# Running dense matmuls as four column groups beside P V, in a fused attention and gated-FFN block

## The chip, the cores and the metric

One core of one Trainium2 chip. The metric is the device time of one execution in microseconds; the times before are the median of three runs. Profiles are of one execution on the same core. TensorE is called PE, its weight loads PEld, ScalarE ACT, VectorE DVE, GpSimd POOL, and SyncE, which issues all DMAs, SP.

## What is computed

One transformer block on x of 2048 tokens and 1024 features, bf16: layernorm, multi-query attention with 32 heads of 32 features that share one key and one value head, a residual, a second layernorm, a gated FFN of width 3584, a second residual.

```python
q = (ln(x) @ wq)            # 2048 x 1024, 32 heads of 32
k = ln(x) @ wk              # 2048 x 32, shared by all heads
v = ln(x) @ wv              # 2048 x 32
p = softmax(q k^T / sqrt(32))
h = x + (p @ v) @ wo
g, u = ln(h) @ w_gate, ln(h) @ w_up       # 2048 x 3584 each
out = h + (sigmoid(g) * u) @ w_down
```

## The kernel before

**Tiles and stages.** Tokens go in 16 tiles of 128. Attention runs over "halves": `hf = 2 * c + hh` is token tile `c` with half `hh` of the heads (16 heads). A *visit* is one half with one tile `kt` of 128 keys; there are 32 x 16 = 512 visits, 32 for each token tile. A visit does:

- **S** (`emit_S`, L687): four matmuls that use 32 rows of the array each, at four row positions, so they run side by side ("row" mode). They write two pairs of banks of `S_ps`; there are three such pairs.
- **exp** (L707): two ACTIVATEs of 128x1024 from `S_ps` to a slot of `Pr`. S of the next visits needs the banks that earlier exps free.
- **acc add** (`make_add`, L680): DVE adds the slot to `acc`, the running sum of P over key tiles, for all halves but the first.

When enough key tiles of a half are there, **P V** (`mk_PV`, L773) multiplies them with `Vt`: for each key tile four matmuls of 32 stationary columns each, at four column positions ("col" mode), all accumulated in one bank of `F_ps`. Such a group is one *part* of the half; `parts_of(hf)` says where the parts are cut. DVE then takes the group out to `oun` (a copy for the first part, L803, an add for each later one, L807). **SUM** (`mk_SUM`, L737) reduces `acc` to row sums with 32 short col-mode matmuls of 64 columns; the reciprocal goes through `r_scratch` in DRAM and comes back to all partitions as `rb`. `OT` is `oun` times `rb` (L765).

The rest of PE's work is "dense" matmuls that use the whole 128x128 array and one of the two banks of `F_ps`: K, V and Q projections (`mk_KV`, `mk_Qc`, `mk_Q`), the output projection (`mk_OP`, L864), gate and up (`mk_GU`, L966: groups of 8 matmuls of 512 columns; for the first and last token tile, 32 matmuls of 128 columns with the weights stationary) and down (`mk_D`, L1044: two groups of 28). Gate ends in a tanh on ACT (L989), up in a multiply on DVE (L1010 or L996).

**Order.** Nothing is ordered by hand on PE. A planner (`Plan`, L48 on) runs when the program is built: it keeps a model of every engine's time and fills PE's list operation by operation. `pe_op` (L447) adds a price `SWITCH` when an operation's mode differs from the one before it; `t_act` (L159) prices an ACTIVATE. The main loop asks, in this order: is the next S known to be ready and ACT close to running dry (`run - t < TUNE["run"]`); if PE is in col mode and S will be ready within `swait`, wait for it; may a P V, SUM, OP or layernorm-transpose group interrupt the current long dense group (if at least `rmin` ns of that group are left); else the next matmul of the current group; else a new group by the priority list `PRIOS`. `in_row(few)` (L734) is the gate of P V and SUM: they begin only in row mode, that is, right after an S, or when few slots are free.

All PE instructions other than layernorm transposes are recorded by one helper, so they stand at L445.

**After the last exp.** With no S left, PE runs the rest alone: the last P V and row sums, the last output projection, gate/up of the last token tile, and the last down groups.

The row-mode gate that the change touches:

```python
def in_row(few):
    return v_done[0] >= NV or pl.pe_mode == "row" or len(free_slots) <= few or TUNE["col_ok"] and pl.pe_mode == "col"
```

Of the kernel before, what the change touches and what calls it, by code (L numbers as in the profile page):

```python
# [17 lines left out]

TUNE = dict(early=240, look=500, ln_v=1, warm=70, late=300, ws0=1, ws1=1, parts0=3, parts1=4, lord=2, h_ord=2,
            ho=3, ho2=0, pvl1=0, pvl2=0, col_ok=0, pace0=310, swait=400, parts=2, raw=1, rl=0, nd=2, pc=16,  # L20
            rate=315, pace=265, xd=4, qf=1, dall=1, wo_late=1, nkn=3, few=0, rmin=900, hmin=1, h0=100, h1=250,
            hf=1.35, run=700, sum_few=0, pv_few=4, d_off=0, d_a=-1, d_b=1, eb=450, eq=1500)


# [134 lines left out]
def t_act(n):  # L159
    return dict(occ=n / 1.2 + 58.0, lat=n / 1.2 + 186.0 + SEM)  # L160

# [4 lines left out]

SWITCH = 108.0


def bass_sequential_preLN__grouped_kv_mqa__glu_gated_glu__prompt_kernel(  # L170
# [31 lines left out]
    with ExitStack() as es:  # L202
# [238 lines left out]
        head = [["xT", "KV", "Q0"], ["KV", "Q0", "xT"], ["Q0", "KV", "xT"], ["KV", "xT", "Q0"]][TUNE["h_ord"]] + ["PV", "SUM", "OP", "hT"]  # L441
        PRIOS = [head + ["GU", "D", "Q1", "Q"], head + ["Q1", "Q", "GU", "D"], head + ["Q1", "GU", "Q", "D"]]

        def mm(o, l, r, start, stop, **kw):
            return lambda: PE.matmul(o, lhsT=l, rhs=r, start=start, stop=stop, **kw)  # L445

        def pe_op(fn, n, mode, deps, last_of_round=True):  # L447
            if mode != pl.pe_mode:
                pl.free["pe"] += SWITCH
                pl.pe_mode = mode  # L450
            if mode == "dense":
                occ = max(25.0, n / 2.4 + 2.4)
            else:
                occ = max(25.0, n / 2.4 + 2.4) - 10.5 if last_of_round else 3.5
            return pl.op("pe", fn, deps, occ=occ, lat=max(25.0, n / 2.4 + 2.0) + 170.0 + SEM)
# [51 lines left out]
        def mk_KV(t0, k):  # L507
            n = k * P
            blk, o = t0 // 4, (t0 % 4) * P

            def atoms(b):
                r = []
                for dt in range(DT):
                    r.append((mm(F_ps[:, b, 0:n], wk4[:, dt, :], xnT[:, blk, dt, o:o + n], dt == 0, dt == DT - 1),
                              n, "dense", rep_ops if dt == 0 else []))
                for x in range(k):
                    for dt in range(DT):
                        r.append((mm(F_ps[:, b, 256 + x * DH:256 + (x + 1) * DH],
                                     xnT[:, blk, dt, o + x * P:o + (x + 1) * P], wv_sb[:, dt, :],
                                     dt == 0, dt == DT - 1), DH, "dense", [wv_ld] if dt == 0 else []))  # L520
                return r

            def after(b, last):
                blk_done(blk, last)
                fa, fd = both(kT4[:, t0 * P:t0 * P + n], F_ps[:, b, 0:n])
                ke = evac(fa, fd, n, [last], 1, bias=TUNE["eb"])
                fa, fd = both(Vt[:, t0:t0 + k, :], F_ps[:, b, 256:256 + k * DH].rearrange("p (a b) -> p a b", a=k))
                ve = evac(fa, fd, k * DH, [last, ke], 2, bias=TUNE["eb"])
                for t in range(t0, t0 + k):
                    k_ev[t], v_ev[t] = ke, ve  # L530
                return [ke, ve]
            return Group("KV", atoms, lambda: [xT_ev.get(t0), xT_ev.get(t0 + k - 1), rep_ops[-1], wv_ld], after)
# [27 lines left out]
        def mk_Qc(c, qd):  # L560
            def atoms(b):
                return [(mm(F_ps[:, b, k * P:(k + 1) * P], wq_sb[:, qd, dt, k * P:(k + 1) * P],
                            xnT[:, 0, dt, c * P:(c + 1) * P], dt == 0, dt == DT - 1), P, "dense", [])
                        for k in range(2) for dt in range(DT)]
# [11 lines left out]
        def mk_Q(g, tok, n):  # L576
            def atoms(b):
                return [(mm(F_ps[:, b, 0:n], wq_sb[:, g // 2, dt, (g % 2) * P:(g % 2 + 1) * P],
                            xnT[:, tok // 512, dt, tok % 512:tok % 512 + n],
                            dt == 0, dt == DT - 1), n, "dense", []) for dt in range(DT)]  # L580
# [75 lines left out]
        def s_known(v, t):  # L656

            sd = s_ready(v)
            return sd is not None and known(sd, t) and (v < 1 or known([exps[2 * v - 2]], t + TUNE["early"]))

# [61 lines left out]

        PARTS = [(), (), (0, 8, 16), (0, 5, 10, 16), (0, 6, 11, 16), (0, 4, 8, 12, 16), (0, 7, 16), (0, 6, 16), (0, 4, 10, 16), (0, 4, 8, 16)]

        def parts_of(hf):
            return PARTS[TUNE["parts" if hf > 1 else "parts0" if hf == 0 else "parts1"]]

# [6 lines left out]
        def in_row(few):  # L734
            return v_done[0] >= NV or pl.pe_mode == "row" or len(free_slots) <= few or TUNE["col_ok"] and pl.pe_mode == "col"

        def mk_SUM(hf):  # L737
            a = acc[:, hf % 2, :]

            def atoms(b):  # L740
                return [(mm(F_ps[DH * j:DH * (j + 1), b, 0:64], sel[:, bb, :], a[:, j * 512 + bb * 64:j * 512 + (bb + 1) * 64],
                            bb == 0, bb == 7, tile_position=(0, DH * j)), 64, "col" if j == 3 else "col-", [])
                        for bb in range(8) for j in range(4)]

            def after(b, last):
# [9 lines left out]
                return [rc]  # L755
            return Group("SUM", atoms, lambda: [add_op.get((hf, NT - 1)), c_sel], after, lambda: in_row(TUNE["sum_few"]))

# [15 lines left out]
        def mk_PV(hf, part, sums=False):  # L773
# [38 lines left out]

            lag = TUNE["pvl2"] if final else TUNE["pvl1"]

            def first():
                return [exp_of[(hf, kt, i)] for kt in kts[:len(kts) - lag] for i in range(2)] + [c_one if sums else v_ev.get(kt) for kt in kts]

            def gate():
                if part == 0 and hf >= 2 and not (hf - 2 in ot_ev and known([ot_ev[hf - 2]], pl.free["pe"])):
                    return False  # L820
                if sums and part == 0 and hf >= 2 and hf - 1 not in ot_ev:
                    return False
                return (hf in RAW or all((hf, max(kt, 1)) in add_op for kt in kts)) and in_row(TUNE["pv_few"])
            return Group("PV", atoms, first, after, gate)
# [39 lines left out]
        def mk_OP(t, dc):  # L864
            def atoms(b):
                return [(mm(F_ps[:, b, :], OT[:, g, :], wo_sb[:, g, dc * 512:(dc + 1) * 512], g == 0, g == NG - 1),
                         512, "dense", []) for g in range(NG)]
# [98 lines left out]
        def mk_GU(t, i):  # L966
# [6 lines left out]
            def atoms(w):  # L973
                def a(b):
                    us, ops = slab_at[(t, i, w)]
                    if held_w:
                        return [(mm(F_ps[:, b, k * P:(k + 1) * P], us[dt // 4][:, dt % 4, k * P:(k + 1) * P], hnT[:, dt, t % 2, :],
                                    dt == 0, dt == DT - 1), P, "dense", [ops[dt // 2]] if k == 0 and dt % 2 == 0 else [])
                                for k in range(4) for dt in range(DT)]
                    return [(mm(F_ps[:, b, :], hnT[:, dt, t % 2, :], us[dt // 4][:, dt % 4, :], dt == 0, dt == DT - 1),  # L980
                             512, "dense", [ops[dt // 2]] if dt % 2 == 0 else []) for dt in range(DT)]
# [62 lines left out]
        def mk_D(p, t, dq):  # L1044
# [4 lines left out]
            def atoms(b):  # L1049
                return [(mm(F_ps[:, b, 0:DW], hv[:, ft, t % 2, :], wd_sb[:, ft, sl], k == 0, k == NFT - 1), DW, "dense",  # L1050
                         ([hact_ev[(t, ft)]] if dq == 0 else []) + ([wd_ld[ft]] if t == 0 and dq == 0 else []))
# [35 lines left out]
        def all_done(v):  # L1087

            v_done[0] = v
            if v == NV:  # L1090
                all_S[0] = True
                pl.t_last = pl.free["pe"]
                load_next([(s.rearrange("p (d f) -> p d f", d=4), rel) for s, rel in free_slots])

        def known(deps, t):
            return all(d is not None and d.end is not None and d.end <= t for d in deps)

        while True:
# [15 lines left out]
            if v < NV:  # L1114
# [3 lines left out]
                can_s = s_known(v, t)  # L1118
                if can_s and run - t < TUNE["run"]:
                    emit_S(v)  # L1120
# [4 lines left out]
                if pl.pe_mode == "col" and not can_s and not (  # L1125
                        cur is not None and cur[1][cur_i][2] != "dense") and s_known(v, t + TUNE["swait"]) and run - t < TUNE["run"] + TUNE["swait"]:

# [4 lines left out]
            if cur is not None and not held and cur[0].cls in LONG and known(bank_rel[1 - cur_b], t):  # L1132

                for cl in ("PV", "SUM", "OP", "hT"):
                    if queues[cl] and (v >= NV or len(free_slots) <= TUNE["few"] or cl == "PV" and pl.pe_mode == "row" or (
                            len(cur[1]) - cur_i) * max(25.0, cur[1][cur_i][1] / 2.4 + 2.4) >= TUNE["rmin"]):
                        gr = queues[cl][0]
# [7 lines left out]
            if cur is not None:  # L1145
                at = cur[1][cur_i]
                if known(at[3], t):
                    mode = at[2]
                    o = pe_op(at[0], at[1], "col" if mode == "col-" else mode, at[3] + (cur[2] if cur_i == 0 else []),
                              mode != "col-")  # L1150
                    if len(at) > 4 and at[4] is not None:
# [10 lines left out]
            else:  # L1162
                pick = None
                banks = [b for b in range(2) if known(bank_rel[b], t)]
                if banks:
                    pr = PRIOS[TUNE["qf"]]
                    if d_due and len(queues["GU"]) <= d_due[0] + TUNE["d_off"]:
                        pr = PRIO_D
# [134 lines left out]
```

## Time and profile before

| | us |
|---|---|
| median of 3 runs | 1092.59 |
| lowest, highest run | 1092.07, 1093.51 |
| span of the profiled execution | 1092.9 |
| PE busy | 1060.6 |
| ACT busy | 1000.7 |
| DVE busy | 848.9 |
| first S starts | 13.74 |
| last S starts | 1007.27 |

The profiled execution's own time is its span, 1092.9 us, 0.3 us above the median. It is 1092.9 us from the first to the last instruction. Busy time is the union of the engine's instructions; PE's and ACT's are pipelined, so a short wait between two of them can be covered by the tail of the earlier one. Start-to-start times within a run of equal instructions tell what one costs.

### The profile page before, as it was taken

The numbers are of one execution on the slowest core, as the hardware profiler recorded it, in microseconds if no ns is written. First come the engines' busy times: TensorE is split into PE (matmuls) and PEld (weight loads), VectorE is DVE, ScalarE is ACT, GpSimd is POOL, SyncE is SP. The second block draws the span as 40 slices with busy tenths as digits, with TensorE's granted clock in tenths as the row PEclk, the third lists the DMA queues.
The fourth block names the chain that finished last, engine by engine and source line by source line (L and its number), as shares of the span: only waits on it lengthen the run. The fifth ranks groups of instructions, "written<-read, shape, count | busy, mean of one in ns | idle before, by whom it ended". The sixth has DMA issues, their size and how long they took to land.

```text
span 1092.9 us, 23470 instructions
## 1 busy us (share of the span) xinstructions
PE 1060.6 (97%) x9314; PEld 439.3 (40%) x9454; DVE 848.9 (78%) x1054; ACT 1000.7 (92%) x1152; POOL 39.5 (4%) x61
## 2 busy tenths in 40 slices
PE   8999999999999999999999999999999999999998
PEld 6533465333333333333333333333333333333485
DVE  8989988787887878787887878787887878787311
ACT  4999999999999999999999999999999999999010
POOL 3300000000000000000000000000000000000000
PEclk9999999999999999999999999999999999999999
DMA  8893399868769595868858595877858586876992
GB/s 248 171 306 121 116 300 279 251 170 269 203 182 266 137 271 144 246 183 255 231 166 256 139 270 147 260 189 229 245 150 262 138 250 168 248 206 194 287 307 95
DMA packets 296509, 233.70 MB, mean 214 GB/s; under 512 B 99536, under 2 KB 282832, under 8 KB 296400
## 3 DMA queue, kind: packets, MB, share of 16 engines
q1 hardware_dynamic: 296400, 232.19, 74.1%
q8 instruction: 75, 1.23, 0.5%
q14 instruction: 34, 0.28, 0.1%
HBM read 203.82 MB, written 8.12 MB: 194 GB/s over the span
## 4 chain that ended last, share of the span: by engine, by line
ACT 67%; PE 22%; issue 5%; DVE 3%; DMA 2%; SPq 0%; DVEq 0%
ACT Pr L707 62%; PE F_ps L445 19%; ACT tnh L989 5%; PE S_ps L445 3%; DVE acc L680 1%; DMA hnT<-hn 1%; DMA r_scratch<-r_sb 1%; DMA zone<-ring 0%; DVE st L349 0%; DVE st L351 0%; DMA ring<-in_A_x_dram 0%; DMA rb<-r_scratch 0%; DVE hact L285 0%; DVE ring L393 0%; DVE OT L765 0%
## 5 line engine op out<-in xcount | busy, mean ns | idle before, releaser
L707 ACT ACTIVATE Pr<-S_ps 128x1024 bf16<-128x1024 f32 x1008 | 956.1, 1181 | 3.4 <-PE S_ps L445 3.4
L680 DVE TENSOR_TENSOR acc<-acc,Pr 128x2048 bf16<-128x2048 bf16 x431 | 524.7, 1217 | 45.4 <-ACT Pr L707 32.1
L445 PE MATMUL F_ps<-ring,hnT 128*128 128x512 bf16 x1506 | 366.8, 380 | 4.4 <-issue 4.1
L445 PE MATMUL F_ps<-zone,hact 128*128 128x512 bf16 x813 | 212.1, 381 | 6.5 <-issue 4.3
L445 PE MATMUL S_ps<-QTb,kT 32*128 32x512 bf16 x2048 | 206.8, 385 | 5.6 <-ACT Pr L707 4.7
L445 PEld LDWEIGHTS F_ps<-ring,hnT 128*128 128x128 bf16 x1536 | 134.6, 98 | 180.8 <-issue 43.0
L989 ACT ACTIVATE tnh<-F_ps 128x512 f32<-128x512 f32 x112 | 83.7, 747 | 60.3 <-PE F_ps L445 60.3
L445 PEld LDWEIGHTS S_ps<-QTb,kT 32*128 32x128 bf16 x2048 | 53.7, 91 | 205.0 <-ACT Pr L707 123.9
L445 PE MATMUL F_ps<-Pr,Vt 128*32 128x512 bf16 x2016 | 134.1, 382 | 0.0
L445 PEld LDWEIGHTS F_ps<-zone,hact 128*128 128x128 bf16 x896 | 75.5, 97 | 104.0 <-issue 34.6
L1010 DVE SCALAR_TENSOR_TENSOR act_s<-tnh,F_ps 128x512 bf16<-128x512 f32 x98 | 67.2, 686 | 58.4 <-PE F_ps L445 58.3
L445 PE MATMUL F_ps<-zone 128*128 128x512 bf16 (+3 forms) x573 | 72.9, 272 | 4.3 <-DVE ring L393 1.0
L445 PEld LDWEIGHTS F_ps<-Pr,Vt 128*32 128x32 bf16 x2016 | 43.0, 95 | 68.0 <-issue 28.6
L445 PE MATMUL F_ps<-wo_sb,OT 128*128 128x512 bf16 x241 | 62.3, 381 | 2.5 <-issue 1.7
L367 POOL TENSOR_TENSOR dsb<-zb,cst 128x1 bf16<-128x1 bf16 x18 | 23.0, 1280 | 964.6 <-DVE zb L364 964.6
L1057 DVE SCALAR_TENSOR_TENSOR h_sb<-F_ps,h_sb 128x512 bf16<-128x512 f32 x32 | 22.1, 692 | 40.4 <-PE F_ps L445 40.3
L445 PEld LDWEIGHTS F_ps<-zone 128*128 128x128 bf16 x584 | 39.0, 97 | 31.3 <-issue 9.2
L680 DVE TENSOR_TENSOR acc<-Pr 128x2048 bf16<-128x2048 bf16 x31 | 37.9, 1224 | 9.7 <-ACT Pr L707 9.7
L445 PE MATMUL F_ps<-hnT,ring 128*128 128x128 bf16 x576 | 37.7, 223 | 0.7 <-ACT tnh L989 0.7
L807 DVE TENSOR_TENSOR oun<-F_ps,oun 128x512 f32<-128x512 f32 x34 | 23.4, 688 | 18.9 <-PE F_ps L445 18.8
L445 PEld LDWEIGHTS F_ps<-hnT,ring 128*128 128x128 bf16 x576 | 33.6, 100 | 6.7 <-issue 5.9
L445 PEld LDWEIGHTS F_ps<-wo_sb,OT 128*128 128x128 bf16 x256 | 21.3, 97 | 34.0 <-issue 12.5
(81 smaller groups left out, 350.9 us busy)
## 6 DMA issues: line engine op xcount, KB each, us to landing
ring<-in_B_w_gate_dram SPq DMA_DIRECT2D x308, 256.0 KB, 3.9
ring<-in_B_w_up_dram SPq DMA_DIRECT2D x308, 256.0 KB, 4.0
rb<-r_scratch SPq DMA_DIRECT2D x124, 64.0 KB, 2.0
zone<-in_B_w_down_dram SPq DMA_DIRECT2D x14, 512.0 KB, 4.5
Pr<-in_B_w_gate_dram SPq DMA_DIRECT2D x20, 256.0 KB, 5.4
Pr<-in_B_w_up_dram SPq DMA_DIRECT2D x20, 256.0 KB, 5.0
ring<-in_A_x_dram SPq DMA_DIRECT2D x16, 256.0 KB, 6.4
h_sb<-in_A_x_dram SPq DMA_DIRECT2D x16, 256.0 KB, 2.9
```

The source lines that it names most:

```text
L367: g = pl.op("pool", lambda: POOL.tensor_tensor(out=dsb[:, ph, tk], in0=zb[:, ph, tk], in1=half[:, 0:k], op=ALU.pow), [f, c0], prio=0, **sl ...
L445: return lambda: PE.matmul(o, lhsT=l, rhs=r, start=start, stop=stop, **kw)
L680: add_op[(hf, kt)] = pl.op("dve", lambda: DVE.tensor_tensor(out=a, in0=in0, in1=slot, op=ALU.add), dp, prio=6, occ=1135, lat=1255)
L707: exps[u] = pl.op("act", lambda i=i, pb=pb: ACT.activation(out=slot[:, i * 1024:(i + 1) * 1024].rearrange("p (a b) -> p a b", a=2), in_=S_ ...
L807: oun_ev[(hf, part)] = pl.op("dve", lambda: DVE.tensor_tensor(out=o, in0=F_ps[:, b, :], in1=o, op=ALU.add), [last, oun_ev[(hf, part - 1)]] ...
L989: box["a"] = pl.op("act", lambda: ACT.activation(out=tnh[:, :], in_=F_ps[:, b, :], func=ACTF.Tanh, scale=0.5), [last, box.get("e")], prio= ...
L1010: e = pl.op("dve", lambda: DVE.scalar_tensor_tensor(out=so, in0=tnh[:, :], scalar=1.0, in1=F_ps[:, b, :], op0=ALU.add, op1=ALU.mult), [las ...
L1057: e = pl.op("dve", lambda: DVE.scalar_tensor_tensor(out=h_sb[:, t % NHB, sl], in0=F_ps[:, b, 0:DW], scalar=0.5, in1=h_sb[:, t % NHB, sl], ...
```

## The change

- `wide` gives a dense matmul a second form: four matmuls of 32 stationary columns each (`quads`), at the four column positions, all with the same moving operand, writing the four quarters of the same output partitions. All dense groups but the V projection and the transposes get it.
- `stay_col` decides which form is used, when the planner places the matmul: the four-fold form if PE is in col mode, or in row mode with visits left and a P V or SUM group queued.
- `in_row` lets P V begin in col mode too (`few` is 4); SUM may begin in any mode (`sm=2`).
- The halves from the third on are cut at key tiles 2, 9 and 16 (parts of 2, 7 and 7) instead of 8 and 16.
- Any P V, SUM, OP or transpose group may interrupt a long dense group however little is left of it (`rmin=0`), PE does not wait in col mode for a coming S (`swait=0`), and new dense groups are picked in the order `Q1, Q, GU, D` (as before).
- The planner's prices change: a mode change by the mode it leaves (106.5, 111, 114 instead of 108 ns), an ACTIVATE of n columns n/1.2 + 50.7 instead of n/1.2 + 58.

```diff
-            ho=3, ho2=0, pvl1=0, pvl2=0, col_ok=0, pace0=310, swait=400, parts=2, raw=1, rl=0, nd=2, pc=16,
+            ho=3, ho2=0, pvl1=0, pvl2=0, col_ok=0, pace0=310, swait=400, parts=11, raw=1, rl=0, nd=2, pc=16,
...
+KN = dict(early=240, keep=0, few=4, lag=0, rmin=0, pri=0, swait=0, sm=2, run=700)
...
-    return dict(occ=n / 1.2 + 58.0, lat=n / 1.2 + 186.0 + SEM)
+    return dict(occ=n / 1.2 + 50.7, lat=n / 1.2 + 186.0 + SEM)
...
-SWITCH = 108.0
+SWITCH = {"dense": 106.5, "row": 111.0, "col": 114.0}
...
+        def wide(o, l, r, start, stop):
+            f = mm(o, l, r, start, stop)
+            f.quads = [(lambda j=j: PE.matmul(o[DH * j:DH * (j + 1)], lhsT=l[:, DH * j:DH * (j + 1)], rhs=r, start=start,
+                                              stop=stop, tile_position=(0, DH * j))) for j in range(4)]
+            return f
...
-                pl.free["pe"] += SWITCH
+                pl.free["pe"] += SWITCH[pl.pe_mode]
...
-                return [(mm(F_ps[:, b, 0:n], wq_sb[:, g // 2, dt, (g % 2) * P:(g % 2 + 1) * P],
+                return [(wide(F_ps[:, b, 0:n], wq_sb[:, g // 2, dt, (g % 2) * P:(g % 2 + 1) * P],
...
-        PARTS = [(), (), (0, 8, 16), (0, 5, 10, 16), ...]
+        PARTS = [(), (), (0, 8, 16), (0, 5, 10, 16), ..., (0, 2, 9, 16), ...]
...
         def in_row(few):
-            return v_done[0] >= NV or pl.pe_mode == "row" or len(free_slots) <= few or TUNE["col_ok"] and pl.pe_mode == "col"
+            return v_done[0] >= NV or pl.pe_mode == "row" or few > 0 and pl.pe_mode == "col" or len(free_slots) <= few
...
+        def stay_col():
+            return pl.pe_mode == "col" or pl.pe_mode == "row" and v_done[0] < NV and bool(queues["PV"] or queues["SUM"])
...
                 if known(at[3], t):
                     mode = at[2]
-                    o = pe_op(at[0], at[1], "col" if mode == "col-" else mode, at[3] + (cur[2] if cur_i == 0 else []),
-                              mode != "col-")
+                    dp = at[3] + (cur[2] if cur_i == 0 else [])
+                    if mode == "dense" and hasattr(at[0], "quads") and stay_col():
+                        for j in range(4):
+                            o = pe_op(at[0].quads[j], at[1], "col", dp if j == 0 else [], j == 3)
+                            o.tag = cur[0].cls
+                    else:
+                        o = pe_op(at[0], at[1], "col" if mode == "col-" else mode, dp, mode != "col-")
```

## The prediction

> **What bounds the kernel now.** First the page: busy shares and the chain that ended last.
>
> ```profile
> span 1092.9 us, 23470 instructions
> PE 1060.6 (97%) x9314; PEld 439.3 (40%) x9454; DVE 848.9 (78%) x1054; ACT 1000.7 (92%) x1152; POOL 39.5 (4%) x61
> ACT 67%; PE 22%; issue 5%; DVE 3%; DMA 2%; SPq 0%; DVEq 0%
> ```
>
> PE and ACT are both full. The chain names ACT, but an average cannot say which of two full engines makes the other wait. So next the table by stages, cut at one token tile (32 visits, 64 exps, 7 tanhs) to the next:
>
> ```profile
> 388.67:450.76 62.09, 60.89 (x496) 22.18 (x505) 50.14 (x57) 62.09 (x72) 1.46 (x1) 1.00 0.75 215
> 450.76:512.86 62.10, 60.90 (x496) 22.19 (x505) 50.00 (x57) 62.10 (x73) 1.45 (x1) 1.00 0.74 207
> ```
>
> Columns: window, length, busy us of PE, weight loads, DVE, ACT, POOL, clock, DMA share, GB/s. A tile takes 62.10 us, and from exp 192 to exp 1024 thirteen tiles repeat this. DVE is at 50 us: not the bound. "Busy" hides short waits in pipelined work, so I price each engine's tile by start-to-start times. PE's timeline:
>
> ```profile
> 496.76 0.40 PE L445 MATMUL S_ps<-QTb,kT 32*128 32x512 bf16 x4
> 497.08 1.04 PE L445 MATMUL F_ps<-ring,hnT 128*128 128x512 bf16 x4
> 498.05 0.61 PE L445 MATMUL F_ps<-Pr,Vt 128*32 128x512 bf16 x8
> 498.60 0.39 PE L445 MATMUL S_ps<-QTb,kT 32*128 32x512 bf16 x4
> 498.92 1.48 PE L445 MATMUL F_ps<-Pr,Vt 128*32 128x512 bf16 x24
> 500.33 0.39 PE L445 MATMUL S_ps<-QTb,kT 32*128 32x512 bf16 x4
> ...
> 502.28 0.39 PE L445 MATMUL S_ps<-QTb,kT 32*128 32x512 bf16 x4
> 502.61 2.12 PE L445 MATMUL F_ps<-ring,hnT 128*128 128x512 bf16 x9
> 504.65 0.40 PE L445 MATMUL S_ps<-QTb,kT 32*128 32x512 bf16 x4
> 504.98 1.47 PE L445 MATMUL F_ps<-ring,hnT 128*128 128x512 bf16 x6
> 506.38 0.39 PE L445 MATMUL S_ps<-QTb,kT 32*128 32x512 bf16 x4
> ```
>
> Nine dense matmuls last 2.12, one 0.39: (2.12 - 0.39)/8 = 0.216 each. S with six of them (504.65 to 506.38) takes 1.73, so an S with its two changes of array mode costs 1.73 - 6 x 0.216 = 0.434: one round of 0.216 and 0.109 a change. S with six rounds of P V (24 matmuls, 498.60 to 500.33) takes the same 1.73: four column-group matmuls of 32 columns cost what one dense matmul costs. S with four dense and two P V (496.76 to 498.60) takes 1.84: the dense-to-column change inside costs another 0.11. ACT's timeline:
>
> ```profile
> 63.90 2.06 ACT L707 ACTIVATE hnT<-S_ps 128x1024 bf16<-128x1024 f32 x2
> 65.71 2.09 ACT L707 ACTIVATE QTb<-S_ps 128x1024 bf16<-128x1024 f32 x2
> 67.52 2.11 ACT L707 ACTIVATE hact<-S_ps 128x1024 bf16<-128x1024 f32 x2
> ```
> ```profile
> 503.63 0.74 ACT L989 ACTIVATE tnh<-F_ps 128x512 f32<-128x512 f32 x1
> 504.11 3.93 ACT L707 ACTIVATE Pr<-S_ps 128x1024 bf16<-128x1024 f32 x4
> 507.81 0.71 ACT L989 ACTIVATE tnh<-F_ps 128x512 f32<-128x512 f32 x1
> ```
>
> Undisturbed, two exps take 1.81 (0.904 each); a tanh holds ACT 0.48. The four exps in the second fence take (507.81 - 504.11)/4 = 0.925: they wait a little for S.
>
> The tile by engine. ACT: 64 x 0.904 + 7 x 0.48 = 61.2. PE: 32 S x 0.434 = 13.9; 184 dense (112 gate/up, 56 down, 16 output projection) x 0.216 = 39.7; 32 P V rounds x 0.216 = 6.9; 16 row-sum rounds x 0.03 = 0.5; and 9 changes between dense and column mode x 0.11 = 1.0 (the built order has 73 changes a tile, 64 of them around S). Sum 62.0. The tile takes 62.10: **PE is the bound, by 0.8 us a tile, and ACT is next at once.**
>
> **The change, part by part.**
>
> 1. *Column-mode dense work.* In the built order 1996 dense matmuls become four each, 5988 more matmuls and as many loads. Mode changes between the first and last S fall from 1162 to 1028; in a steady tile from 73 to 64, two an S, so every dense/column change is gone. PE's tile: 62.0 - 9 x 0.11 = 61.0, 0.15 under ACT's 61.2.
>
> The four-fold rounds of 512 columns I cost at 0.216, the P V row. For 685 rounds of 128 columns (237 with the first token tile's gate/up, 448 in the tail) these rows count:
>
> ```profile
> 455.97 0.42 PE L445 MATMUL F_ps<-acc,sel 128*32 128x64 bf16 x32
> ```
> ```profile
> 59.95 0.44 PE L445 MATMUL F_ps<-zone 128*128 128x32 bf16 x11
> 1062.74 3.74 PE L445 MATMUL F_ps<-hnT,Pr 128*128 128x128 bf16 x64
> ```
>
> A dense one takes (3.74 - 0.2)/63 = 0.056. Row sums put four loads and four 64-column matmuls through in (0.42 - 0.20)/7 = 0.031 a round, so 0.056 should hold. The other bound: short dense matmuls run at (0.44 - 0.18)/10 = 0.026 a load-and-matmul pair; four in series would be 0.104. I take 0.057, since the row-sum row has the same form.
>
> [...]
>
> 2. *P V in three parts (2, 7, 7 key tiles) instead of two.* Same P V rounds; 30 more accumulations into oun on DVE at 0.688 (two a tile, 1.4 us): 50.1 becomes 51.5 of 61, so covered by DVE's slack. If that cover failed, a bank of F_ps would stay taken behind an acc add of 1.22: bounds per extra group 0 and 1.2 + 0.7. I take 0, because DVE idles 10 us a tile.
>
> 3. *Gates and planner numbers.* P V and SUM may start in any mode and interrupt a dense group with little left; PE no longer idles up to 0.4 us in column mode for a coming S. The planner's exp price becomes 853 + 50.7 = 904 ns, which is the ACT row, instead of 911; so S is placed at the cadence ACT can keep. These edits only move order. SP's list keeps its 1021 DMAs; no queue gains a wait. ACT takes one small copy of Vt from DVE (0.2 us).
>
> 4. *Steady tiles.* PE 61.0 against ACT 61.2: two engines that close, with three exps of buffer, do not run at the larger sum alone. Bounds 61.2 (all waits gone) and 62.1 (they only change place); I take 61.5, as before the tile stood 0.1 over the larger sum with 0.8 between the engines. Gain 0.6 x 13 = 7.8 (0 to 11.7).
>
> 5. *First three tiles* (to exp 192) take 64.3, 59.4 and 64.7; their changes fall from 73, 72, 71 to 69, 64, 64: 19 x 0.109 = 2.1 if PE-bound, but loads, layernorm and a half-clock stretch sit here. I take a gain of 1 (-2 to 2).
>
> 6. *Tail.* From the last S (1007.27) PE is nearly alone. Three more down rounds and one P V round fewer: +0.43; three mode changes fewer: -0.3; 448 rounds at +0.001: +0.5. Sum +0.6 (0 to +22).
>
> Sum: -7.8 - 1 + 0.6 = -8.2; 1092.9 - 8.2 = 1084.7 in a profiled run. The runs' median, 1092.59, lies 0.3 under that span: **1084.4 us**.
>
> **Rivals.**
>
> *No gain (1090.4 to 1094.8).* The saved changes become PE waits: S cannot be issued before the exp that frees its banks. For: ACT floor and PE sum are within 1.4%. Against: in the trace, from 260 to 900 us, 154 of 330 exps of a visit's first half start late and 0.04 us after their S ended, so they waited for PE; and PE's sum matched the tile. Steady term 0, tail +0.6: about 1092.5. Chance 0.10.
>
> *Four-fold narrow rounds in series (slower).* In the tail, 448 rounds with 8 instructions each, issue or load bound at 0.104: +0.048 x 448 = +21.5, and 237 x 0.048 = +11.4 of which perhaps a third shows: 1084.4 + 25 = 1109. It decides from 8.2/685 = 0.012 over 0.056, that is, 0.068 a round. The row-sum row is against it; but it shows only bursts of 32. Chance 0.09.
>
> [...]
>
> *P V's extra groups hold a bank (slower).* Both banks of F_ps stand behind DVE more often; PE waits at the next dense group. 30 groups at up to 1.2: 1084.4 + up to 36; it turns the sign from 0.27 a group. Typical 1098. Chance 0.09.
>
> The forecast itself: 0.72.
>
> **How the numbers follow.** A measurement of this kernel can tell about 0.2% (2.2 us) from no change. The forecast's own range is 1079.5 to 1090; with no gain and the cheaper slow outcomes, 1079 to 1096. Faster 0.72, same 0.10, slower 0.18.
>
> **What would show it.** Right: tiles of about 61.5 us; exps at 0.904 to 0.91; in PE's timeline no dense next to P V without an S between, except as column rounds; x36 column matmuls of gate/up with the length of nine dense ones; 128-column rounds at 0.056 in the tail; last S to end near 86 us. Wrong: tiles still near 62.1 with PE waiting for exps (no gain); the tail's 128-column stretches grown by more than a tenth (series); waits of PE for DVE's oun between groups (banks).

## The result and the profile after

| | us |
|---|---|
| before, median of 4 runs (lowest, highest) | 1092.57 (1092.07, 1093.51) |
| after, median of 4 runs (lowest, highest) | 1140.00 (1137.85, 1141.30) |
| after / before, with its 95% interval | 1.0432 (1.0417 to 1.0446) |
| span of the profiled execution, before and after | 1092.9, 1139.5 |

The change makes the kernel 47 us slower. The prediction had the wrong sign, and its range ended at 1096. In every run whose time and profile are both on record, the time is 1.8 us more than the profile's span. The profiled execution of before, with its span of 1092.9, was therefore about 2 us slower than the median; times are compared below with times, and spans with spans. The page of the changed kernel, the lines that answer to those shown of before, then the tenths of the granted clock, the instruction queue and the chain's lines:

```profile
span 1139.5 us, 35630 instructions
PE 1089.6 (96%) x15442; PEld 460.9 (40%) x15442; DVE 868.7 (76%) x1083; ACT 1003.0 (88%) x1153; POOL 40.3 (4%) x61
PEclk9999989999999999999999999999999999999889
q8 instruction: 122, 2.00, 0.7%
PE 74%; ACT 14%; issue 5%; DVE 3%; DMA 2%; SPq 1%; DVEq 0%
```

PE's busy time grew by 29.0 us and its matmuls in the trace from 9314 to 15442; ACT's work is the same. The clock dips in two places, near 160 us and at the end. The same two places stand out when the span is cut at events that both kernels have:

| stretch | before | after | difference |
|---|---|---|---|
| exp 128 to exp 192 (the tile with the first narrow gate/up) | 64.7 | 76.5 | +11.9 |
| mean of the 13 tiles from exp 192 | 62.1 | 62.2 | +1.6 in all |
| everything else up to the last S | | | +0.5 |
| last S to the end | 85.6 | 118.3 | +32.7 |

So 44.6 of the 46.6 us lie where four-fold rounds of 128 columns run, and the 512-column rounds of the steady tiles gave nothing. Two steady tiles in the table by stages (columns as in the prediction):

```profile
463.71:525.77 62.06, 61.79 (x691) 22.83 (x690) 51.53 (x60) 62.06 (x73) 1.45 (x1) 1.00 0.75 206
525.77:588.09 62.32, 62.32 (x745) 23.30 (x741) 51.41 (x59) 62.31 (x73) 1.46 (x1) 1.00 0.75 216
```

The tile is as long as before, and PE is *busier* (60.9 before), although nine mode changes a tile have gone. PE's timeline there:

```profile
509.48 2.13 PE L454 MATMUL F_ps<-ring,hnT 128*32 128x512 bf16 x36
511.54 0.40 PE L450 MATMUL S_ps<-QTb,kT 32*128 32x512 bf16 x4
511.86 0.61 PE L454 MATMUL F_ps<-ring,hnT 128*32 128x512 bf16 x8
512.30 1.03 PE L450 MATMUL F_ps<-Pr,Vt 128*32 128x512 bf16 x16
```

L454 is the four-fold form. Nine four-fold rounds (x36) last 2.13, where nine dense matmuls lasted 2.12, and P V follows gate/up without the extra step of 0.11. Both are as priced. Now the tail:

```profile
1059.00 3.19 PE L454 MATMUL F_ps<-hnT,Pr 128*32 128x128 bf16 x128 [2.95 <-issue]
1063.30 1.97 PE L454 MATMUL F_ps<-hnT,Pr 128*32 128x128 bf16 x128 [1.10 <-issue]
1067.59 1.97 PE L454 MATMUL F_ps<-hnT,Pr 128*32 128x128 bf16 x128 [2.32 <-issue]
1071.34 2.11 PE L454 MATMUL F_ps<-hnT,Pr 128*32 128x128 bf16 x127 [1.77 <-issue]
1076.11 0.34 PE L454 MATMUL F_ps<-hnT,Pr 128*32 128x128 bf16 x9 [2.67 <-issue]
...
1103.16 7.91 PE L454 MATMUL F_ps<-zone,hact 128*32 128x512 bf16 x111 [2.44 <-issue]
```

A round costs nearly what the prediction said (0.057): 128 matmuls in 1.97 are 4 x (1.97 - 0.22)/127 = 0.055 a round. But after every 128 matmuls of these rows PE stands still for 1 to 3 us, and the releaser is "issue": PE waits for no semaphore, engine or data transfer that the profile shows. 128 matmuls with their 128 loads are 256 instructions. The instruction queue q8 moved 122 packets of 2.00 MB/122 = 16.4 KB; PE's matmuls, loads and semaphore waits in the trace are 31337, and 31337/256 = 122.4. In before they are 19186, and 19186/256 = 74.9 with 75 packets (`q8 instruction: 75, 1.23, 0.5%`). One packet (a block, below) is 256 PE instructions. In the trace's records of that queue the packet for the next block lands 1.2 to 1.6 us before PE resumes, each time; from the start of its fetch to the resumption are 2.2 to 2.9 us. PE resumes at 1059.00, 1063.30, 1067.59, 1071.34 and 1076.11: 17.11/4 = 4.28 us for 256 instructions, 60 a microsecond. A four-fold round of 128 columns asks for 8 per 0.056 us, 143 a microsecond; one of 512 columns 8 per 0.216, 37; a dense one of 128 columns 2 per 0.056, 36.

From the tail's first narrow round to the end PE passes 16 ends of a block and stands at 13 of them for 0.6 us or more; all its stands there sum to 23.7 us of the 32.7. Some rounds were slower too: after the longest stand the 128 matmuls took 3.19 instead of 1.97, at a granted clock of 0.63 from 1059 to 1061 us. The stage in numbers:

```profile
1050.00:1139.00 89.00, 62.06 (x2304) 43.83 (x2296) 8.96 (x13) 4.78 (x8) 0.00 (x0) 0.92 0.50 135
```

The clock is 0.92 over the stage (eighth column), where before it was 1.00 from 1050 us on; x1 below, with the same order and no such stands, has 1.00 there too.

### The profile page after: what moved, and what is told of

Same layout as the page of the kernel before. It is cut to its first block, busy times and chain, and to the rows that moved or that the text cites. A ratio compares the mean times of both kernels' runs of the same rounds, so it can differ in the third digit from the quotient of the medians.

```text
span 1139.5 us, 35630 instructions
## 1 busy us (share of the span) xinstructions
PE 1089.6 (96%) x15442; PEld 460.9 (40%) x15442; DVE 868.7 (76%) x1083; ACT 1003.0 (88%) x1153; POOL 40.3 (4%) x61
## 4 chain that ended last, share of the span: by engine, by line
PE 74%; ACT 14%; issue 5%; DVE 3%; DMA 2%; SPq 1%; DVEq 0%
PE F_ps L450 39%; PE F_ps L454 24%; ACT Pr L718 13%; PE S_ps L450 12%; DVE acc L691 1%; ACT tnh L1004 1%; DMA zone<-in_A_wq_dram 1%; DMA hnT<-hn 1%; DVE act_s L1025 0%; DMA ring<-in_B_w_up_dram 0%; DMA r_scratch<-r_sb 0%; SPq L306 0%; DMA rb<-r_scratch 0%; DVE OT L780 0%; DVE oun L822 0%
## 5 line engine op out<-in xcount | busy, mean ns | idle before, releaser
L450 PE MATMUL F_ps<-ring,hnT 128*128 128x512 bf16 x1122 | 273.2, 380 | 0.1
L450 PE MATMUL S_ps<-QTb,kT 32*128 32x512 bf16 x2048 | 210.7, 386 | 3.0 <-issue 1.7
L450 PEld LDWEIGHTS F_ps<-ring,hnT 128*128 128x128 bf16 x1122 | 97.2, 98 | 130.5 <-issue 34.5
L450 PE MATMUL F_ps<-Pr,Vt 128*32 128x512 bf16 x2016 | 142.5, 382 | 4.0 <-issue 1.7
L454 PE MATMUL F_ps<-zone,hact 128*32 128x512 bf16 x2148 | 139.4, 384 | 3.3 <-issue 3.3
L450 PEld LDWEIGHTS S_ps<-QTb,kT 32*128 32x128 bf16 x2048 | 54.3, 91 | 214.3 <-ACT Pr L718 112.3
L454 PE MATMUL F_ps<-ring,hnT 128*32 128x512 bf16 x1656 | 106.5, 381 | 0.1
L1025 DVE SCALAR_TENSOR_TENSOR act_s<-tnh,F_ps 128x512 bf16<-128x512 f32 x98 | 67.2, 686 | 47.4 <-PE F_ps L454 22.4
L450 PE MATMUL F_ps<-zone,hact 128*128 128x512 bf16 x359 | 90.9, 381 | 0.0
L454 PEld LDWEIGHTS F_ps<-zone,hact 128*32 128x32 bf16 x2148 | 55.6, 97 | 58.0 <-issue 15.5
L450 PEld LDWEIGHTS F_ps<-Pr,Vt 128*32 128x32 bf16 x2016 | 44.6, 95 | 65.9 <-issue 26.3
L822 DVE TENSOR_TENSOR oun<-F_ps,oun 128x512 f32<-128x512 f32 x64 | 44.0, 688 | 33.1 <-PE F_ps L450 32.0
L454 PEld LDWEIGHTS F_ps<-ring,hnT 128*32 128x32 bf16 x1656 | 39.4, 96 | 46.1 <-issue 14.1
L450 PEld LDWEIGHTS F_ps<-zone,hact 128*128 128x128 bf16 x359 | 30.9, 97 | 43.3 <-issue 14.5
L450 PE MATMUL F_ps<-zone 128*128 128x128 bf16 (+3 forms) x420 | 41.2, 246 | 2.3 <-DMA zone<-in_A_wq_dram 1.3
L454 PE MATMUL F_ps<-wo_sb,OT 128*32 128x512 bf16 x656 | 41.3, 380 | 0.6 <-DVE OT L780 0.6
```

The lines of the kernel that those rows point to most:

```text
L454: f.quads = [(lambda j=j: PE.matmul(o[DH * j:DH * (j + 1)], lhsT=l[:, DH * j:DH * (j + 1)], rhs=r, start=start, stop=stop, tile_position=( ...
L822: oun_ev[(hf, part)] = pl.op("dve", lambda: DVE.tensor_tensor(out=o, in0=F_ps[:, b, :], in1=o, op=ALU.add), [last, oun_ev[(hf, part - 1)]] ...
L1025: e = pl.op("dve", lambda: DVE.scalar_tensor_tensor(out=so, in0=tnh[:, :], scalar=1.0, in1=F_ps[:, b, :], op0=ALU.add, op1=ALU.mult), [las ...
```

## The experiments

The theories. **A**: PE waits for its next block of instructions; in its strict form, blocks of 256 cannot be had faster than about one in 4.28 us, and the narrow four-fold rounds ask for more. **B**: the column form itself is slow in narrow rounds. **C**: in the steady tiles the changes are really saved, but the saving turns into waits between S and exp, so that sums over a tile do not tell the gain; **C1** says S only stands too late in the order, **C2** that PE has too much work in some visits whatever the order. Against C stands the prediction's own reckoning, a gain of 8 to 11 us from the saved changes.

**x1_narrow_dense: the changed kernel's own order, its 128-column rounds as one dense matmul.** The planner still plans four pieces; three of them issue nothing, so the order stays.

```diff
+                        whole = at[1] <= P
...
-                            o = pe_op(at[0].quads[j], at[1], "col", dp if j == 0 else [], j == 3)
+                            fn = at[0].quads[j] if not whole else at[0] if j == 3 else (lambda: None)
+                            o = pe_op(fn, at[1], "col", dp if j == 0 else [], j == 3)
```

> The changed kernel's own order of instructions, with the 685 rounds of 128 columns issued as one dense matmul each instead of four column-group ones; all else stays four-fold. Theory A (supply of instructions: in the changed kernel's tail PE runs 128 matmuls and 128 loads in 1.97 us, then stands 1 to 3 us until the next 16 KB page of instructions has landed): the tail goes from 118 us back to about 86, the tile with the narrow gate/up from 76.5 to about 65, total 1139.5 - 32 - 11.5 = 1095 to 1097. Theory B (the four short loads or matmuls of a round are slow in themselves): the same total, so this run only shows that the narrow rounds are the cause; a third theory, that the steady tiles or the 512-column rounds carry the loss, gives 1125 or more.

Measured: 1098.69 (1096.42 to 1100.32), 1.0055 (1.0034 to 1.0075) of before. 41.3 of the 47.4 us are gone. The tile from exp 128 takes 63.3 and the tail 88.2. The tail's timeline:

```profile
1043.45 6.75 PE L450 MATMUL F_ps<-hnT,Pr 128*128 128x128 bf16 x118 [2.29 <-DMA hnT<-hn]
```

118 narrow matmuls now run without one stand, where the changed kernel had one in each 32 rounds. What is left over before is taken up under "what stays open".

**x4_tail_dense: the same with `whole = v_done[0] >= NV`**: everything after the last S is dense, the narrow rounds of the first token tile stay four-fold.

> The changed kernel's own order, four-fold rounds kept while S are left, and everything after the last S dense. Theory A: the tail goes from 118 to about 86, the narrow tile stays at 76.5: total 1139.5 - 32.5 = 1107. If the 512-column rounds of the tail are to blame too, the tail here is shorter than in x1 by more than 1 us; I expect the same within 1 us.

Measured: 1107.95 (1104.89 to 1109.68). The tail accounts for 1140.0 - 1107.95 = 32.0, and the first token tile for 1107.95 - 1098.69 = 9.3. In x4's profile the tail is 83.9 us, 1.7 under before's, and the tile from exp 128 still takes 78.9. The split is not sharp: by the profiles the two places are worth more, 118.3 - 83.9 = 34.4 and 78.9 - 63.3 = 15.6, but x1's tail, at 88.2, is 4.3 longer than x4's, where 1 at most was expected. Of that, 3.5 are waits of x1 for data (0.36, 0.81 and 2.29), and x4 has none over 0.3. Whether the four-fold 512-column rounds in x1's tail bring on such waits, one profile of each cannot tell.

**x2_all_dense: the same with `whole = True`**: no four-fold round anywhere, so every P V in the middle of dense work again pays its change of mode.

> The changed kernel's own order with every four-fold round issued as one dense matmul: the order, the cuts of P V at 2, 9, 16 and the gates stay, the column form goes. Mode changes in a steady tile rise from 64 to 73 to 79 in alternation (76 on average). If a change costs 0.11 us and PE sets the tile: 62.2 becomes 62.9 to 63.3, total x1 plus 9 to 15 us (about 1107). If the column form saved nothing because ACT and the place of S set the tile, x1 plus 0 to 3 us.

Measured: 1104.12 (1103.57 to 1105.14), 5.4 above x1, between the two forecasts. In the profiles the last S starts at 1018.57 against 1008.16 in x1, 10.4 later; x2's shorter tail, 83.8 against 88.2, gives part of it back. The changes have their price:

```profile
504.86 0.83 PE L450 MATMUL F_ps<-Pr,Vt 128*32 128x512 bf16 x12
505.62 1.04 PE L450 MATMUL F_ps<-ring,hnT 128*128 128x512 bf16 x4
506.59 0.40 PE L450 MATMUL S_ps<-QTb,kT 32*128 32x512 bf16 x4
```

From the P V to S are 1.73 us for three rounds and four: 7 x 0.216 = 1.51, and 0.22 for the change inside and the one before S, 0.11 each. Column form is worth its price in *this* order, which puts P V anywhere. What it does in the order of before is the next question.

**y1_before_cols: the kernel before, its order, cuts, gates and planner numbers untouched; only 256- and 512-column dense matmuls that share a stretch between two S with P V or row sums are issued four-fold.** This is the column form alone; mode changes fall from 73 to 64 a tile.

```diff
+        at_S = [i for i, o in enumerate(pe) if o.tag == "S"][::4]
+        for i, k in zip(at_S, at_S[1:]):
+            seg = pe[i + 4:k]
+            rest = [o for o in seg if o.tag not in ("PV", "SUM")]
+            if len(rest) < len(seg) and all(hasattr(o.fn, "quads") for o in rest):
+                for o in rest:
+                    o.fn = o.fn.quads
```

> The kernel before with its own order, cuts, gates and planner numbers; only where P V or row sums stand between two S beside dense matmuls, those dense matmuls (256 and 512 columns) are issued as four column-group ones. Mode changes in a steady tile fall from 73 to 64, PE's sum from 61.7 to 60.8 us, nothing is reordered. Theory C (PE and ACT meet again at every S within about 0.2 us, so time saved in one visit is not lent to another; only visits where ACT was late by PE's doing gain): tiles 61.7 to 62.0 instead of 62.1, total 1 to 6 us under the kernel before. The prediction's way of reckoning (the larger of the two sums of a tile): tiles 61.2 to 61.5, 8 to 11 us under it. If four-fold rounds cost something that was not seen: no gain, or slower.

Measured: 1091.78 (1090.55 to 1092.38, 11 runs) against 1092.63 (17 runs), 0.9990 (0.9981 to 0.9999). The whole gain is 0.85 us; the reckoning by sums is refuted. C named the reason but also expected too much, 1 to 6 us and tiles of 61.7 to 62.0. The tile is still exactly 62.10:

```profile
388.04:450.14 62.10, 60.94 (x575) 23.24 (x583) 50.31 (x57) 62.10 (x72) 1.46 (x1) 1.00 0.83 216
```

The timeline shows where the saved changes go:

```profile
327.39 0.40 PE L445 MATMUL S_ps<-QTb,kT 32*128 32x512 bf16 x4
327.72 1.05 PE L445 MATMUL F_ps<-Pr,Vt 128*32 128x512 bf16 x16
328.59 0.39 PE L445 MATMUL F_ps<-zone,hact 128*32 128x512 bf16 x4
328.92 0.55 PE L445 MATMUL S_ps<-QTb,kT 32*128 32x512 bf16 x4
...
330.80 0.50 PE L445 MATMUL S_ps<-QTb,kT 32*128 32x512 bf16 x4
...
332.67 0.47 PE L445 MATMUL S_ps<-QTb,kT 32*128 32x512 bf16 x4
```

Between the first two S five rounds cost 328.92 - 327.39 = 1.53; the change inside is gone. But S itself then lasts 0.55, 0.50 and 0.47 instead of 0.39: its second half has to wait, by the program, for the exp that frees its banks, and the profile counts these 0.08 to 0.16 as busy. In the trace of before four S between 326 and 574 us are as long (0.50, the first at 331.35); the third matmul of each starts 0.055 after an exp has ended. Visits with P V shrink from 1.84 to 1.74 and the ones after them grow, most of them from 1.94 to between 1.97 and 2.05. PE can run ahead of ACT only as far as the three pairs of banks go, so what one visit saves is not kept for the next that is too long.

**x3_s_early: x1 with the S of 64 visits moved ahead of one 0.216 us round**, in visits whose exps started late.

```diff
+        for s in EARLY_S:
+            i = at_S[s]
+            a, b = pe[i - 1], pe[i + 4]
+            n = 4 if form(a) == "col" else 1
+            back = pe[i - n:i]
+            if a.tag != "SUM" and form(a) == form(b) and all(o.tag == a.tag for o in back):
+                pe[i - n:i + 4] = pe[i:i + 4] + back
```

> x1_narrow_dense with S of 64 late visits (those whose first exp began over 0.03 us late in x1, where the round ahead of S has the form of the round behind it) moved ahead of that one round of 0.216 us; the work is the same, mode changes 64 a tile as in x1. Theory C1 (S only stands in the wrong place by part of a round): the lateness of these visits goes, some 0.3 to 0.4 us a tile, 4 to 5 us under x1. Theory C2 (in these stretches PE is busy without a wait and simply has more work a visit than ACT, so the round that S is moved over is late at the next S): within 1.5 us of x1.

Measured: 1098.37 (1097.77 to 1098.85), the same as x1. C1 falls for this shift of S by one round; other placements were not tried. C2 agrees with the result, but nothing tests it by itself.

**e3_split64: the kernel before, every narrow gate/up matmul as two dense ones of 64 columns.** Twice the instructions, no column mode.

```diff
-                                    dt == 0, dt == DT - 1), P, "dense", [ops[dt // 2]] if k == 0 and dt % 2 == 0 else [])
-                                for k in range(4) for dt in range(DT)]
+                                    dt == 0, dt == DT - 1), 64, "dense", [ops[dt // 2]] if k == 0 and z == 0 and dt % 2 == 0 else [])
+                                for k in range(4) for z in range(2) for dt in range(DT)]
```

> The kernel before, with each dense 128-column gate/up matmul of the first and last token tile issued as two dense ones of 64 columns: no column mode anywhere near it, twice the instructions. Theory A: 4 instructions in 0.058 us is 69 a us, over the 256 in about 4.3 us (60 a us) that the pages gave in the changed kernel's tail: stands of PE of roughly 0.3 to 1 us, always at the same place of the page, and narrow stretches about 10% longer than 0.058 a pair, +2 to +5 us in the tail. Theory B: no such stands, +1 us. The planner makes another order of it, so its total says little (1090 to 1100).

Measured in a single run: 1105.56. PE's timeline after the last S:

```profile
1044.54 4.74 PE L445 MATMUL F_ps<-hnT,Pr 128*128 128x64 bf16 x157
1051.30 3.06 PE L445 MATMUL F_ps<-hnT,Pr 128*128 128x64 bf16 x99 [2.02 <-issue]
1054.20 0.98 PE L445 MATMUL F_ps<-hnT,ring 128*128 128x64 bf16 x28
1057.07 5.09 PE L445 MATMUL F_ps<-hnT,ring 128*128 128x64 bf16 x116 [1.90 <-issue]
```

The whole array, dense mode, and the same stands, 256 instructions apart, with PE resuming 1.6 and 1.4 us after the packet landed. B is out as their cause. The first row's 64-column matmuls start every (4.74 - 0.2)/156 = 0.029 us, so PE asks for 2/0.029 = 69 instructions a microsecond. The stands, 2.02 and 1.90, are longer than expected, and rarer: PE stands at 2 of the 8 block ends in the narrow stretches. From 1069.45 to 1076.91 us 256 narrow matmuls, 512 instructions, run at the same 69 a microsecond without any. The strict form of A forecasts neither: at 60 a microsecond each block would lose some 0.6 us. The tail takes 95.9 us, 10.3 more than before, of which the two stands are 3.9; the rest was not separated from the new order.

**e4_split32: the same with four dense matmuls of 32 columns** (`32 * z`, `range(4)`): as many instructions as in the changed kernel, and still no column mode.

> The kernel before, with every 128-column gate/up matmul of the first and last token tile issued as four dense matmuls of 32 columns: four times the instructions, as in the changed kernel, but no column mode anywhere in them. After the last S that is 448 x 4 x 2 = 3584 instructions of load and matmul, 14 blocks of 256. Theory A (PE's instructions come in blocks of 256 that are not to be had faster than one per 4.28 us): these 14 blocks take 14 x 4.28 = 59.9 us instead of 448 x 0.056 = 25.1, so the stretch from the last S to the end grows from 85.6 by about 35 to 117 to 122, as in the changed kernel (118.3), with stands of PE at the same place of each block; and with some of the first tile's share the run takes 1135 to 1155. Theory B (the stands belong to the column form, and dense matmuls run at their own pace): the shortest dense load-and-matmul pair of the kernel before starts every 0.026 us, so 1792 of them take 46.6 us, the stretch grows by 21.5 to about 107, without stands, and the run takes 1114 to 1125.

Measured in a single run: 1157.0, more than either theory said. The narrow rounds run from 1066.57 to 1134.20 with one down group of 5.8 between:

```profile
1079.53 6.32 PE L445 MATMUL F_ps<-hnT,ring 128*128 128x32 bf16 x230 [2.91 <-issue]
1085.69 4.19 PE L445 MATMUL F_ps<-hnT,Pr 128*128 128x32 bf16 x152
1092.80 3.50 PE L445 MATMUL F_ps<-hnT,Pr 128*128 128x32 bf16 x127 [2.92 <-issue]
1098.56 6.38 PE L445 MATMUL F_ps<-hnT,Pr 128*128 128x32 bf16 x233 [2.26 <-issue]
```

That is 61.8 us, where A said 59.9 and B 46.6. B's 46.6 and stands of 13.7 us make up nearly all of it, so PE waits for blocks here too; that the sum comes close to A's is partly luck. PE stands at 7 of 15 block ends, not at each, and the 382 matmuls from 1079.53 to 1089.88, three blocks, run at 74 instructions a microsecond without a stand. One block in 4.28 us is no ceiling.

The fetches in e3 and e4 show what goes with a stand. When the fetch of the next block starts 1.1 to 1.5 us after PE resumed, as it does after five of these nine stands of 0.3 us or more, PE stands at the next block end for 0.37 us or not at all. When it starts 2.7 to 4.0 us after, the next stand is 1.9 to 2.9 us. The long stands go with a late start of the fetch; why some start late is open.

The forecast for the whole run missed because the planner prices the smaller matmuls differently and builds another order: the last S starts at 1017.13, 9.9 later, and the rest of the tail is 138.0 - 61.8 = 76.2 us, where before has 85.6 - 25.1 = 60.5. Only the narrow stretch is evidence.

**v1_replanned: an attempt at a better version.** The changed kernel with narrow gate/up dense, P V cut at 8 and 16, and other planner numbers.

```diff
-            ho=3, ho2=0, pvl1=0, pvl2=0, col_ok=0, pace0=310, swait=400, parts=11, raw=1, rl=0, nd=2, pc=16,
+            ho=3, ho2=0, pvl1=0, pvl2=0, col_ok=0, pace0=310, swait=400, parts=2, raw=1, rl=0, nd=2, pc=16,
-            hf=1.35, run=700, sum_few=0, pv_few=4, d_off=0, d_a=-1, d_b=1, eb=450, eq=1500)
+            hf=1.35, run=700, sum_few=0, pv_few=4, d_off=1, d_a=-1, d_b=1, eb=450, eq=1500)
-KN = dict(early=240, keep=0, few=4, lag=0, rmin=0, pri=0, swait=0, sm=2, run=700)
+KN = dict(early=280, keep=0, few=4, lag=0, rmin=900, pri=0, swait=0, sm=2, run=740)
-                        return [(wide(F_ps[:, b, k * P:(k + 1) * P], ...
+                        return [(mm(F_ps[:, b, k * P:(k + 1) * P], ...
```

> A version meant to beat both: the changed kernel with narrow rounds dense, P V cut at 8 and 16 again, interrupts as before the change (rmin 900), S allowed a little earlier (early 280, run 740) and down groups one step later (d_off 1); the planner makes a new order, 64 changes a tile, PE's sum 60.9. If theory A names the main loss and P V's three parts most of the rest: no stands of PE at page ends, tiles 61.4 to 61.8, total 1078 to 1088. If the column form or the gates are to blame for the rest: 1090 to 1098.

Measured: 1095.87 (1094.48 to 1098.67), 1.0035 (1.0023 to 1.0047), with tiles of 62.04 to 62.15. The stands in the tail are gone, but the 1078 to 1088 that were expected without them did not come. None of the orders brings the mean steady tile under 62.0. The only version below before is y1.

**What stays open.** x1 is 5.8 us above before though it has no stands and fewer changes. The profiles show 3.4 of that (before's was of an execution above its median): 0.9 lies before the last S and 2.5 behind it, in waits for hnT and for gate and up weights; but x2 and x4, with the same order and dense rounds there, have tails of 83.8 and 83.9, under before's 85.6. Which part of the order (three P V parts, the open gates, the planner's numbers) costs the rest was not separated. What decides when PE's next block is fetched was not tried either.

## Why the prediction was wrong

**Terms 1 and 6, the narrow rounds: the step that failed.** The prediction took 0.057 for a 128-column round "since the row-sum row has the same form". The form was right and so is the price, 0.055. But the row-sum row is a burst of 32 matmuls with their loads, 64 instructions, a quarter of a block, so it could not show what 448 rounds in a row need. The sum had 0.5 us for the tail's 448 rounds and nothing for the first token tile's 237; x4 and x1 measure 32.0 + 9.3 = 41.3. In the place of the 0.057 stood rounds of 0.055 and, between them, waits of PE for its next block of instructions. The upper bound of +22 for the tail failed for the same reason: it was taken from the pace of a load-and-matmul pair, 0.104 a round, again from a burst (11 matmuls). The changed kernel needs 52.5 us between its first and last narrow matmul without the down groups, against 25.1 for the same rounds dense at 0.056. At the densest stretch's pace they would take 3584/256 x 4.28 = 59.9; that the down matmuls between them, at 37 instructions a microsecond, let the fetch catch up would explain the difference, but was not tested. The stands inside and behind the down groups (2.44 and 0.88) come on top.

The count that gave it away was in the prediction: "5988 more matmuls and as many loads", and the page had the queue's 75 packets. What was missing was the division by time: 8 instructions per 0.056 us, four times the 36 a microsecond at which the dense rounds were known to run.

**Term 1, the 512-column rounds.** Right: 0.216 a round, 0.11 a change, 64 changes a tile. x2 shows their worth in this order: 5.4 us of the time, 10.4 up to the last S.

**Term 4, the steady tiles.** −7.8 was forecast, +1.6 came. "As before the tile stood 0.1 over the larger sum" read an agreement of 62.0 with 62.10 as the bound. The sum over a tile hides that visits are uneven: five to nine rounds, 1.5 to 2.4 us, against ACT's 1.81 for two exps, with no more than the three pairs of banks to even them out. y1 takes nine changes out of each tile in an unchanged order, and the tile stays at 62.10. That was the second step that failed. The rival "no gain" named this mechanism; its argument against itself, exps that start 0.04 us after S, is true of the late visits only, and the early ones wait inside S.

**Term 2, P V in three parts; term 3, gates.** DVE's tile went from 50.1 to 51.5 as reckoned. A price for the bank was not isolated; in the trace PE's loads for `F_ps` (L450) wait for the `oun` adds (L822) 18 times, at most 0.4 us and 5.0 us in all.

**Term 5** forecast −1 for the first three tiles. The first takes 65.3 (64.3 before), the second 58.9 (59.4), and the third carries the 11.9.

**The last step of the sum.** From the span of 1084.7 the prediction took 0.3 off for the runs' median. By the 1.8 us between time and span it should have added; this is far too small to matter.

**The rivals.** "Four-fold narrow rounds in series" had the place and the sign, and 1109. It left open whether issue or loads would bound the rounds; its price, one pair after another at 0.104 a round, is refuted by the 0.055. The mechanism that decided, PE's wait for its next block of instructions, had neither price nor chance in the prediction. It should have been a rival of its own with a price: an unknown rate, asked for at four times what the trace shows, has no upper bound near zero.

The trace of before has the same blocks. In its tail, where the narrow dense rounds ask for 36 instructions a microsecond, the longest stand put down to "issue" is 0.16 us; in the changed kernel's tail the stands are 0.6 to 3 us at 13 of 16 block ends.

## What to carry to other kernels

When a change multiplies instructions, divide them by the time in which they are to run and compare with the fastest *long* stretch of the trace, not with a short burst; here 36 and 37 a microsecond ran freely in x1's tail, 69 and 74 stood still at some block ends and not at others, and 143 at nearly all. Splitting dense matmuls into column groups cost nothing at 512 columns and 41 us at 128. Where two engines hand over through a few buffers, add up visit by visit: in y1 the buffers did not carry the saving of one visit over to the next that was too long, and of 8 to 11 us reckoned 0.85 came.

## What the hardware showed

- PE's instructions came in packets of 256 (16.4 KB). Asking for 143 a microsecond, PE got one per 4.28 us in the densest stretch; between single resumptions of adjoining blocks 3.4 to 4.9 us. In e4 it ran three in a row at 74 a microsecond.
- PE resumed 1.2 to 1.6 us after the packet had landed, in the changed kernel, in e3 and in e4. The wait appears as "issue", at block ends but not at every one, in column and in dense mode.
- Among stands of 1 to 3 us the granted clock was 0.92 over the last 89 us; x1, with the same order and no such stands, had 1.00 from 1050 us on.
- A 128x128 dense matmul, two of 64 columns and a four-fold round of 32 stationary columns cost nearly the same while instructions last: 0.056, 0.058 and 0.055 us.
